# Regrouping normalised rows through DRAM and transposing them on VectorE, in a one-core transformer block kernel

## The chip, the cores and the metric

The kernel runs on one core of a Trainium2 chip. The metric is the device time of one execution in microseconds (us). Before the change it is 309.4 us, the median of 3 runs (308.99 to 310.95). A core has five engines with a queue of instructions each: TensorE (PE; its weight loads are shown as PEld), VectorE (DVE), ScalarE (ACT), GpSimd (POOL) and SyncE (SP). SP issues nearly all transfers of this kernel. Each engine takes its instructions in order, so an instruction that waits for a semaphore holds back all those behind it.

## The reference

x has 2048 rows (sequence) of 640 features, in bf16. The rows are normalised, and two branches work on the same normalised rows; the result is the sum of x and both.

```python
xn = _layernorm(x, axis=-1)
return x + _A_ref(xn, A_wqkv, A_wo) + _B_ref(xn, B_w_gate, B_w_up, B_w_down)
```

Branch A is attention with 32 heads of 20 features, where each query sees itself and the 255 keys before it, followed by a product with wo. Branch B is `(sigmoid(xn @ w_gate) * (xn @ w_up)) @ w_down` with 1536 hidden features. All the first products (q, k, v, gate, up) contract over the 640 features, so TensorE needs the normalised rows transposed: features on partitions, rows along the free axis.

## The kernel before

The sequence is cut into four chunks of 512 rows (CW), each chunk into four blocks of 128 rows (SBC). The transposed rows of a chunk are a tile `xnT` of 128 partitions x 5 slices (DC) x 512 rows. In the kernel before, slice d on partition p holds feature 128d + p, and the weights are loaded with the same order of their rows (L143, L182).

Chunk 0 is normalised and transposed at the start, with PE transposes (`transpose_rows`, L276 to L280). For chunks 1 to 3, `g_norms` (L343 to L359) is a generator: four steps of statistics on DVE (L252, L258), one power on POOL for all four blocks (L264), a gap of some steps, and four steps that normalise one block each on DVE (`norm_block`, L270). `turn_block` (L282) then gives each block to a transposing DMA on SP's queue, straight into `xnT`. Chunk 3 turns its blocks in a generator of its own (`g_turns`, L361).

The order of all work is laid down when the program is built. Attention steps (scores on PE L487, exponential on ACT L493, mask on POOL L504 or DVE L497, value product on PE L520, its transposes on DVE L532 and L548) come in a fixed list. Between them the class `Fill` (L551) pulls pieces of the other work out of a list of generators (L689 to L707), each with an estimated cost. `mix(a, b, first, every)` runs generator b beside a: from a's step `first` on, after each `every` of a's steps it takes one step of b. So the norms of chunk 1 run beside the gate and up products of chunk 0 ("gu0a", "gu0b"), those of chunk 2 beside the output product of chunk 0 ("out0"), and those of chunk 3 beside "gu1b" and "out1". Directly after each of these comes the q and k projection of the chunk ("qk1", "qk2", "qk3").

What stands on SP's queue around chunk 1 is, in this order: the four turns, the load of x for chunk 2 (`load_x(2)`, L140), eight transfers that turn wo inside DRAM (L212), five loads of wd (L205), two transfers that clear pads of the q and k scratch (L178), the stores of the q projection (L305, with the loads of wo, L217, after the fourth), the stores of the k projection (L305), and the loads that spread q and k over partitions (L315).

The buffers that matter:

- x of a chunk (`xc`) has one buffer for all chunks (pool `xp`, one buffer), read by the statistics and the norms.
- `st`, the projection results on their way to DRAM, has six buffers (pool `stp`); a chunk writes ten, five for q by DVE (L301) and five for k by ACT (L303).
- The accumulators of q, k, v, gate, up, the value product and the output product share four PSUM banks (pool `ps_d`); the scores have one tile of four banks (`ps_s`).
- The normalised block `xn` has four buffers.

Of the kernel before, what the change touches and what calls it, by code (L numbers as in the profile page):

```python
# [9 lines left out]
P = 128  # L10
S = 2048
D = 640
# [3 lines left out]
DC = D // P  # L16
FC = F // P
CW = 512
NCH = S // CW
SBC = CW // P  # L20
# [6 lines left out]
FS = 768  # L27
# [10 lines left out]
BF16 = mybir.dt.bfloat16  # L38
# [55 lines left out]
def kernel(  # L94
# [11 lines left out]
    nc = tc.nc  # L106
# [28 lines left out]
    xc = {}  # L135
# [4 lines left out]
        nc.sync.dma_start(out=t, in_=xr[:, c * SBC:(c + 1) * SBC, :])  # L140

    wqkv = [const.tile([P, DC, D], BF16, name="w" + part) for part in "qkv"]
    wqkv_r = A_wqkv.rearrange("(c p) n -> p c n", p=P)  # L143
    wg = [const.tile([P, DC, FS], BF16, name=f"wg{k}") for k in range(F // FS)]
    wu = [const.tile([P, DC, FS], BF16, name=f"wu{k}") for k in range(F // FS)]
    wd = const.tile([P, FC, D], BF16, name="wd")
# [32 lines left out]

    def load_gu(t, w, k, lo=0, hi=FS):  # L180
        nc.sync.dma_start(out=t[k][:, :, lo:hi],
                          in_=w.rearrange("(c p) f -> p c f", p=P)[:, :, k * FS + lo:k * FS + hi])  # L182

    load_gu(wg, B_w_gate, 0, 0, FS // 2)
    load_gu(wu, B_w_up, 0, 0, FS // 2)
    clear("q", 0)
    clear("k", 0)
    load_gu(wg, B_w_gate, 0, FS // 2)

    def load_rest():  # L190
# [30 lines left out]
    ident = const.tile([P, P], BF16, name="ident")  # L221
# [24 lines left out]
    xnT = {}  # L246
    xns = {}
# [13 lines left out]
    def ln_block(c, s, mv=None):  # L261
        return ln_mv(ln_half(c, s, 1, ln_half(c, s, 0)), mv)

    def rstd_blocks(mvs):  # L264
        rstds = lnp.tile([P, SBC], FP32, name="rstds", bufs=1)
        nc.gpsimd.tensor_scalar(out=rstds, in0=mvs[:, :, 1], scalar1=EPS, scalar2=None, op0=ADD)
        nc.gpsimd.tensor_tensor(out=rstds, in0=rstds, in1=neghalf, op=POW)
        return rstds

    def norm_block(c, s, mv, rstd):  # L270
        xn = lnp.tile([P, D], BF16, name="xn")
        nc.vector.tensor_scalar(out=xn, in0=xc[c][:, s, :], scalar1=mv[:, 0:1],  # L272
                                scalar2=rstd[:, 0:1], op0=SUB, op1=MULT)
        xns[c, s] = xn

    def transpose_rows(s, copy, lo=0, hi=DC):  # L276
        pt = ps_h.tile([P, DC, P], BF16, name="pt", tag="h")
        for d in range(lo, hi):
            nc.tensor.transpose(pt[:, d, :], xns[0, s][:, d * P:(d + 1) * P], ident)  # L279
        copy(out=xnT[0][:, lo:hi, s * P:(s + 1) * P], in_=pt[:, lo:hi, :])  # L280

    def turn_block(c, s):  # L282
        nc.sync.dma_start(out=xnT[c][:, :, s * P:(s + 1) * P], in_=xns.pop((c, s)), transpose=True)

    def new_xnT(c):
        xnT[c] = xtp.tile([P, DC, CW], BF16, name="xnT")
# [53 lines left out]

    MM = 216

    def g_norms(c, turn, gap=3):  # L343


        new_xnT(c)
        mvs = lnp.tile([P, SBC, nc.vector.BN_AGGR_DIM], FP32, name="mvs", bufs=1)
        for s in range(SBC):
            ln_block(c, s, mvs[:, s, :])
            if s == SBC - 1:  # L350
                rstds = rstd_blocks(mvs)
            yield 0
        for _ in range(gap):
            yield 0
        for s in range(SBC):
            norm_block(c, s, mvs[:, s, :], rstds[:, s:s + 1])
            yield 0
            if turn:
                turn_block(c, s)  # L359

    def g_turns(c):  # L361
        for s in range(SBC):
            turn_block(c, s)
            yield 0

    def g_qk(c):
        for w in "qk":
            for m in range(DC):
                proj_block(w, c, m)
                if c == 0 and w == "q" and m == 1:  # L370
                    load_x(1)
                if c == 0 and w == "q" and m == 3:
                    load_gu(wu, B_w_up, 0, FS // 2)
                if c == 1 and w == "q" and m == 3:
                    load_wo()
                if c and w == "k" and m == DC - 1:
                    spread("q", c, 0, GH)
                yield 5 * MM
        if c == 0:
            spread("q", c, 0, 2)  # L380
            spread("k", c, 0, 2)
            spread("q", c, 2, 4)
            spread("k", c, 2, 4)
# [19 lines left out]
    def part(w, d, f):  # L403
        k, first = divmod(f * P, FS)
        return w[k][:, d, first:first + P]

    def g_gu(c, f0, f1):
        for f in range(f0, f1):
            pg = ps_d.tile([P, CW], FP32, name="pg", tag="d")
            for d in range(DC):  # L410
                nc.tensor.matmul(pg, lhsT=part(wg, d, f), rhs=xnT[c][:, d, :],  # L411
                                 start=(d == 0), stop=(d == DC - 1))
            th = tp.tile([P, CW], FP32, name="th")
            nc.scalar.activation(out=th, in_=pg, func=TANH, scale=0.5)  # L414
            yield 5 * MM
            pu = ps_d.tile([P, CW], FP32, name="pu", tag="d")
            for d in range(DC):
                nc.tensor.matmul(pu, lhsT=part(wu, d, f), rhs=xnT[c][:, d, :],  # L418
                                 start=(d == 0), stop=(d == DC - 1))
            h = hp.tile([P, CW], BF16, name="h")  # L420
            ht[c, f] = h
            nc.vector.scalar_tensor_tensor(out=h, in0=th, scalar=1.0, in1=pu, op0=ADD, op1=MULT)  # L422
            yield 5 * MM
# [6 lines left out]
    def down(c, s, y, cut):  # L430
        for f in range(FC):
            nc.tensor.matmul(y[:, 0:cut[1] - cut[0]], lhsT=ht[c, f][:, s * P:(s + 1) * P],  # L432
                             rhs=wd[:, f, cut[0]:cut[1]], start=(f == 0), stop=False)
            if f % 6 == 5:
                yield 6 * 136
# [11 lines left out]
    def new_rows(c, s, name="rows", bufs=3, queue=nc.sync):  # L447
        rows = lnp.tile([P, D], BF16, name=name, bufs=bufs)
        queue.dma_start(out=rows, in_=xr[:, c * SBC + s, :])
        return rows  # L450
# [5 lines left out]
    def outp(c, s, ys, rows):  # L456
        for y, cut in zip(ys, HALVES):
            add_wo(c, s, y, cut)
        for y, cut in zip(ys, HALVES):
            add_x(y, cut, rows)  # L460
        store(c, s, rows)

    def g_out(c, between, ahead=()):
        nxt = new_rows(c, 0)
        for s in range(SBC):
            rows = nxt
            if s == 0:
                yield from ahead
            if s + 1 < SBC:
                nxt = new_rows(c, s + 1)  # L470
            ys = [ps_d.tile([P, CW], FP32, name=f"y{i}", tag="d") for i in range(2)]
            for y, cut in zip(ys, HALVES):
                yield from down(c, s, y, cut)
            if s == 0:
                yield from between
            outp(c, s, ys, rows)
            yield 10 * 136
# [117 lines left out]
    def mix(a, b, first, every=1, rest=True):  # L595

        for k, cost in enumerate(a):
            yield cost
            if k >= first and (k - first) % every == 0:
                yield next(b, 0)  # L600
        if rest:
            yield from b
# [39 lines left out]
    for lo, hi in ((0, 3), (3, DC)):  # L642
        transpose_rows(0, act, lo, hi)
    norm_act(1, xn1, neg1, r1)
    mv3 = ln_mv(ln_half(0, 3, 1, stats3))
    transpose_rows(1, dve)
    v00 = project_v(0, 0, 0)
    r3 = root(mv3)
# [3 lines left out]
    v10 = project_v(0, 1, 0)  # L652
    copy_v(0, 0, 0, v00, dve, (0,))
    transpose_rows(3, dve)
    v01 = project_v(0, 0, 1)
    norm_act(2, xn2, neg2, r2)
# [20 lines left out]
    fill = Fill()  # L677
    GU = 10 * MM
    OUT = 4 * 34 * 136
    APART = 1800  # L680
    FIRST_PART = 1000
    def later(load, *args):
        load(*args)
        yield 0

    norms1 = g_norms(1, True)
    norms2 = g_norms(2, True)
    norms3 = g_norms(3, False, 6)
    fill.add("gu0a", mix(g_gu(0, 0, 4), norms1, 4, 1, False), 4 * GU)  # L689
    fill.add("gu0b", mix(g_gu(0, 4, 12), norms1, 0), 8 * GU)  # L690
    fill.add("x2", later(load_x, 2), 0)
# [7 lines left out]
    fill.add("qk2", g_qk(2), 50 * MM)  # L699
    fill.add("v2", mix(g_v(2), g_gu(1, 3, 7), 0, 1), 40 * 136 + 4 * GU)  # L700
    fill.add("gu1b", mix(g_gu(1, 7, 12), norms3, 0, 1, False), 5 * GU)
    fill.add("out1", mix(g_out(1, g_gu(2, 0, 1)), itertools.chain(norms3, g_turns(3)), 1, 2), OUT + GU)
    fill.add("qk3", g_qk(3), 50 * MM)
    fill.add("v3", mix(g_v(3), g_gu(2, 1, 5), 0, 1), 40 * 136 + 4 * GU)
    fill.add("gu2", g_gu(2, 5, 12), 7 * GU)
# [13 lines left out]
    for t, (c, k, o, step) in enumerate(todo):  # L719
# [11 lines left out]
        pt, late = scores(c, o, step)  # L731
# [12 lines left out]
    c = NCH - 1  # L744
# [6 lines left out]
    rows = [new_rows(c, s, *home, queue=nc.scalar) for s, home in enumerate(homes)]  # L751
# [55 lines left out]
```

## Time and profile before

| | us |
|---|---|
| median of 3 runs | 309.4 |
| lowest and highest run | 308.99, 310.95 |
| span of the profiled execution, first to last instruction | 307.5 |
| PE busy | 299.6 |
| ACT busy | 198.4 |
| DVE busy | 170.7 |
| POOL busy | 169.3 |

The profiled execution's own time is known by its span alone; what lies around the span, start and end of the execution, is not shown, and the median lies 1.9 us above it. The profile's page gives the busy time of each engine, the span in 40 slices, the chain of work that ended last and the costliest groups of instructions. A timeline line gives the start, the length, the engine, the line in the code, the operation, output and inputs, shapes, the number of instructions merged into the line, and in brackets the idle time before it with what ended it. "SPq" marks the issue of a transfer on SP's queue: the length there is that of the issue, not of the transfer.

### The profile page before, as it was taken

To read this page: it belongs to the slowest core of one execution; us is meant where nothing else is said; L and a number is where in the kernel's file an instruction comes from. 1 tells how busy PE (TensorE), PEld (TensorE's weight loads), DVE (VectorE), ACT (ScalarE), POOL (GpSimd) and SP (SyncE) were. 2 spreads that over 40 slices of the span, in tenths; PEclk is the share of its full clock that TensorE was granted. 3 is DMA by queue.
4 is the path that set the end of the run, shared out by engine and by line. 5 is a ranking of instruction groups with operands and counts; after the bars stand their busy time and mean duration, and the time that the engine had idled before them with its cause. 6 is when DMAs were issued, how large, how long until landed. Compare 5 with 4: busy or idle time off the path is not lost.

```text
span 307.5 us, 9944 instructions
## 1 busy us (share of the span) xinstructions
PE 299.6 (97%) x4276; PEld 167.5 (54%) x4311; DVE 170.7 (56%) x339; ACT 198.4 (65%) x197; POOL 169.3 (55%) x308
## 2 busy tenths in 40 slices
PE   7999999999999999999999999999999999999995
PEld 3654444555657654554457654554546664444774
DVE  5633666639698364487946164392824536363523
ACT  6933877698855649888674547878585547687000
POOL 6000686787874828576683729467372937566000
PEclk9999999999999999999999999999999999999999
DMA  7997976986407352820002712730000200000202
GB/s 215 366 344 236 324 158 214 337 238 209 154 2 139 58 179 68 272 83 2 3 3 67 129 58 87 250 122 0 5 0 2 87 26 21 2 2 7 83 21 67
DMA packets 40460, 35.68 MB, mean 116 GB/s; under 512 B 10560, under 2 KB 39872, under 8 KB 40384
## 3 DMA queue, kind: packets, MB, share of 16 engines
q1 hardware_dynamic: 39552, 34.27, 37.3%
q10 hardware_dynamic: 864, 0.77, 0.9%
q8 instruction: 34, 0.56, 0.8%
q14 instruction: 10, 0.08, 0.1%
HBM read 23.63 MB, written 10.26 MB: 110 GB/s over the span
## 4 chain that ended last, share of the span: by engine, by line
PE 96%; issue 1%; DMA 1%; DVE 1%; ACT 0%; SPq 0%
PE y L432 18%; PE pu L418 17%; PE pg L411 17%; PE pqk L297 14%; PE ps L487 9%; PE pv L326 7%; PE y L439 7%; PE acc L520 6%; DMA xc<-in_A_x_dram 1%; PE pt L279 0%; ACT xn L617 0%; DVE xn L272 0%; DVE xn L628 0%; SPq L156 0%; DVE stats L252 0%
## 5 line engine op out<-in xcount | busy, mean ns | idle before, releaser
L504 POOL TENSOR_SCALAR_AFFINE_SELECT pT<-pT 64x512 bf16<-64x512 bf16 (+1 forms) x256 | 157.7, 616 | 108.1 <-ACT pT L493 95.6
L493 ACT ACTIVATE pT<-ps 128x2048 bf16<-128x2048 f32 (+1 forms) x76 | 141.0, 1855 | 59.6 <-PE ps L487 54.6
L422 DVE SCALAR_TENSOR_TENSOR h<-th,pu 128x512 bf16<-128x512 f32 x48 | 32.8, 684 | 52.6 <-PE pu L418 46.1
L418 PE MATMUL pu<-xnT,wu 128*128 128x512 bf16 x228 | 59.0, 380 | 0.7 <-issue 0.2
L411 PE MATMUL pg<-xnT,wg 128*128 128x512 bf16 x226 | 58.5, 380 | 0.9 <-issue 0.3
L432 PE MATMUL y<-wd,h 128*128 128x320 bf16 (+2 forms) x396 | 56.7, 295 | 0.0
L432 PEld LDWEIGHTS <-h 128*128 128x128 bf16 x396 | 36.7, 98 | 15.8 <-issue 2.0
L414 ACT ACTIVATE th<-pg 128x512 f32<-128x512 f32 x48 | 28.6, 595 | 15.5 <-PE pg L411 15.4
L411 PEld LDWEIGHTS <-wg 128*128 128x128 bf16 x240 | 22.2, 98 | 25.8 <-issue 1.8
L418 PEld LDWEIGHTS <-wu 128*128 128x128 bf16 x240 | 22.0, 98 | 25.5 <-issue 2.0
L487 PE MATMUL ps<-qT,kT 20*64 20x320 bf16 (+4 forms) x1440 | 32.1, 260 | 0.0
L532 DVE STREAM_TRANSPOSE t<-acc 128x512 f32<-128x512 f32 x32 | 21.1, 697 | 19.7 <-PE acc L520 19.7
L487 PEld LDWEIGHTS <-kT 20*64 20x64 bf16 x1440 | 15.4, 103 | 24.9 <-issue 21.8
L443 DVE SCALAR_TENSOR_TENSOR rows<-y,rows 128x320 bf16<-128x320 f32 x30 | 14.4, 488 | 25.5 <-PE y L439 25.3
L544 DVE TENSOR_TENSOR on<-t,rec 128x320 bf16<-128x320 f32 (+4 forms) x48 | 27.8, 580 | 1.1
L326 PE MATMUL pv<-wv,xnT 128*128 128x320 bf16 x160 | 25.7, 300 | 0.0
L439 PE MATMUL y<-wo,oc 128*128 128x320 bf16 (+2 forms) x165 | 24.2, 295 | 0.0
L297 PE MATMUL pqk<-xnT,wk 128*128 128x512 bf16 x97 | 23.1, 381 | 0.2
L297 PE MATMUL pqk<-xnT,wq 128*128 128x512 bf16 x94 | 22.8, 381 | 0.4 <-issue 0.2
L335 DVE CAST v<-pv 64x320 bf16<-64x320 f32 x29 | 14.1, 486 | 12.5 <-PE pv L326 12.3
L520 PE MATMUL acc<-pT,v 64*32 64x320 bf16 (+4 forms) x1440 | 19.7, 253 | 0.0
L520 PEld LDWEIGHTS <-v 64*32 64x32 bf16 x1440 | 16.2, 91 | 5.8 <-ACT pT L493 1.7
(50 smaller groups left out, 178.7 us busy)
## 6 DMA issues: line engine op xcount, KB each, us to landing
qT<-sq SPq DMA_DIRECT2D x16, 256.0 KB
kT<-sk SPq DMA_DIRECT2D x16, 256.0 KB
sq<-st SPq DMA_DIRECT2D x20, 128.0 KB
sk<-st SPq DMA_DIRECT2D x20, 128.0 KB
out_dram<-rows SPq DMA_DIRECT2D x15, 160.0 KB
wg<-in_B_w_gate_dram SPq DMA_DIRECT2D x4, 480.0 KB
wu<-in_B_w_up_dram SPq DMA_DIRECT2D x4, 480.0 KB
xc<-in_A_x_dram SPq DMA_DIRECT2D x3, 640.0 KB
```

The costliest lines, as they stand in the source:

```text
L297: nc.tensor.matmul(ps, lhsT=wt[:, m, :], rhs=xnT[c][:, d, :], start=(d == 0), stop=(d == DC - 1))
L326: nc.tensor.matmul(ps[:, 0:HALF], lhsT=xnT[c][:, d, s * P:(s + 1) * P], rhs=wqkv[2][:, d, hf * HALF:(hf + 1) * HALF], start=(d == 0), stop ...
L411: nc.tensor.matmul(pg, lhsT=part(wg, d, f), rhs=xnT[c][:, d, :], start=(d == 0), stop=(d == DC - 1))
L414: nc.scalar.activation(out=th, in_=pg, func=TANH, scale=0.5)
L418: nc.tensor.matmul(pu, lhsT=part(wu, d, f), rhs=xnT[c][:, d, :], start=(d == 0), stop=(d == DC - 1))
L422: nc.vector.scalar_tensor_tensor(out=h, in0=th, scalar=1.0, in1=pu, op0=ADD, op1=MULT)
L432: nc.tensor.matmul(y[:, 0:cut[1] - cut[0]], lhsT=ht[c, f][:, s * P:(s + 1) * P], rhs=wd[:, f, cut[0]:cut[1]], start=(f == 0), stop=False)
L439: nc.tensor.matmul(y[:, 0:cut[1] - cut[0]], lhsT=oc[c, m][:, s * P:(s + 1) * P], rhs=wo[:, m, cut[0]:cut[1]], start=False, stop=(m == DC - 1))
L487: nc.tensor.matmul(ps[a * U:(a + 1) * U, i, col * U:(col + n) * U], lhsT=qk["k", kc, o // GH][32 * i:32 * i + DH, o % GH + a, kb * U:(kb + ...
L493: nc.scalar.activation(out=pt[:, :, 0:width], in_=ps[:, :, 0:width], func=EXP, scale=SCALE)
L504: nc.gpsimd.affine_select(out=view, in_=view, pattern=[[0, HG], [0, n], [sign, U]], compare_op=GE, fill=0.0, base=base, channel_multiplier ...
L520: nc.tensor.matmul(acc[32 * i:32 * i + 32, q * U:(q + n) * U], lhsT=vt[kb][a * U:(a + 1) * U, u, h * VW:h * VW + 32], rhs=pt[a * U:(a + 1) ...
```

## The change

The transposed rows of chunks 1 to 3 are made in another way, and the order of the features changes: slice d on partition p now holds feature 5p + d. The weights wqkv, w_gate and w_up are loaded in that order, and the PE transposes of chunk 0 read every fifth feature.

For a later chunk, `put_block` stores each normalised block to a scratch in DRAM (two scratches, taken in turn). After the fourth, `regroup` loads it back in four transfers into the chunk's own x buffer `xc`: partition 32b + j gets, for each of the 16 groups t of 32 rows, row 32t + j and its features 160b to 160b + 159, in runs of 320 bytes. Then five instructions on DVE (`turn`, one per slice) transpose 32x32 blocks, reading every fifth element, and write one slice of `xnT` each, 128 x 512. `g_norms` yields `lag` steps between regroup and the turns and one step after each turn. On DVE the turns of chunk 1 stand around the last three h products of chunk 0 (one, two, two), those of chunk 2 around the third pair of row additions of "out0" (one before, four after), those of chunk 3 before, between and after the last two pairs of "out1" (two, two, one). The order on PE, ACT and POOL is that of before.

```diff
-    wqkv_r = A_wqkv.rearrange("(c p) n -> p c n", p=P)
+    wqkv_r = A_wqkv.rearrange("(p c) n -> p c n", c=DC)
...
-                          in_=w.rearrange("(c p) f -> p c f", p=P)[:, :, k * FS + lo:k * FS + hi])
+                          in_=w.rearrange("(p c) f -> p c f", c=DC)[:, :, k * FS + lo:k * FS + hi])
...
-            nc.tensor.transpose(pt[:, d, :], xns[0, s][:, d * P:(d + 1) * P], ident)
+            nc.tensor.transpose(pt[:, d, :], xns[0, s].rearrange("p (i d) -> p d i", d=DC)[:, d, :], ident)
...
-    def turn_block(c, s):
-        nc.sync.dma_start(out=xnT[c][:, :, s * P:(s + 1) * P], in_=xns.pop((c, s)), transpose=True)
+    xs = [tc.dram_tile([CW, D], BF16, name=f"xs{k}") for k in range(2)]
+
+    def put_block(c, s):
+        nc.sync.dma_start(out=xs[c % 2][s * P:(s + 1) * P, :], in_=xns.pop((c, s)))
+
+    def regroup(c):
+
+        rows = xs[c % 2].rearrange("(t j) (b f) -> b j t f", j=32, b=4)
+        for b in range(4):
+            nc.sync.dma_start(out=xc[c][32 * b:32 * b + 32].rearrange("j s (a f) -> j (s a) f", a=4), in_=rows[b])
+
+    def turn(c, d):
+        nc.vector.transpose(out=xnT[c][:, d, :], in_=xc[c].rearrange("p s (t d) -> p d (s t)", d=DC)[:, d, :])
...
-    def g_norms(c, turn, gap=3):
-
-
-        new_xnT(c)
+    def g_norms(c, gap=3, lag=3):
...
             norm_block(c, s, mvs[:, s, :], rstds[:, s:s + 1])
+            put_block(c, s)
             yield 0
-            if turn:
-                turn_block(c, s)
-
-    def g_turns(c):
-        for s in range(SBC):
-            turn_block(c, s)
+        regroup(c)
+        for _ in range(lag):
+            yield 0
+        new_xnT(c)
+        for d in range(DC):
+            turn(c, d)
             yield 0
...
-    norms1 = g_norms(1, True)
-    norms2 = g_norms(2, True)
-    norms3 = g_norms(3, False, 6)
+    norms1 = g_norms(1)
+    norms2 = g_norms(2)
+    norms3 = g_norms(3, 6, 2)
...
-    fill.add("out1", mix(g_out(1, g_gu(2, 0, 1)), itertools.chain(norms3, g_turns(3)), 1, 2), OUT + GU)
+    fill.add("out1", mix(g_out(1, g_gu(2, 0, 1)), norms3, 1, 2), OUT + GU)
```

## The prediction

> **What bounds the kernel now.** I read the page's busy times and clock first, then the chain of work that ended last.
>
> ```profile
> span 307.5 us, 9944 instructions
> PE 299.6 (97%) x4276; PEld 167.5 (54%) x4311; DVE 170.7 (56%) x339; ACT 198.4 (65%) x197; POOL 169.3 (55%) x308
> PEclk9999999999999999999999999999999999999999
> PE 96%; issue 1%; DMA 1%; DVE 1%; ACT 0%; SPq 0%
> ```
>
> TensorE is busy 97% at full clock, and the chain runs through it for 96%. The table of windows gives PE 264.9 of the 267 us from 13 to 280, so at most 2.1 us are left to win there. The order on PE, ACT and POOL is the same in both kernels. So the change can only matter by making PE wait, and a wait of PE is paid in full. Next I read the stretch where chunk 1 is normalised, turned and projected: first the timeline of the SP queue, then DVE, then ACT and PE.
>
> ```profile
> 39.32 5.27 SPq L283 DMA_TRANSPOSE xnT<-xn  x4
> 44.64 0.70 SPq L140 DMA_DIRECT2D xc<-in_A_x_dram  x1
> 45.40 5.04 SPq L212 DMA_DIRECT2D wo_i<-in_A_wo_dram  x8
> 50.48 4.34 SPq L205 DMA_DIRECT2D wd<-in_B_w_down_dram  x5
> 55.19 0.60 SPq L178 DMA_DIRECT2D sq<-kT  x1
> 56.15 0.56 SPq L178 DMA_DIRECT2D sk<-kT  x1
> 57.24 5.30 SPq L305 DMA_DIRECT2D sq<-st  x4
> 62.60 2.07 SPq L217 DMA_DIRECT2D wo<-wo_i  x4
> 64.76 0.53 SPq L305 DMA_DIRECT2D sq<-st  x1
> ```
>
> One queue, in order: the load of x chunk 2 at 44.64 stands ahead of 3.6 MB of loads and pads, and these stand ahead of chunk 1's q stores.
>
> ```profile
> 50.31 0.29 DVE L544 TENSOR_TENSOR on<-t,rec 128x128 bf16<-128x128 f32 x1
> 50.52 0.68 DVE L422 SCALAR_TENSOR_TENSOR h<-th,pu 128x512 bf16<-128x512 f32 x1
> 51.79 0.69 DVE L422 SCALAR_TENSOR_TENSOR h<-th,pu 128x512 bf16<-128x512 f32 x1 [0.59 <-PE pu L418]
> 54.57 0.69 DVE L422 SCALAR_TENSOR_TENSOR h<-th,pu 128x512 bf16<-128x512 f32 x1 [2.09 <-ACT th L414]
> ```
>
> Here the five new transposes of chunk 1 go: one before the first of these h, two before the second, two before the third.
>
> ```profile
> 65.43 1.08 ACT L303 CAST st<-pqk 128x512 bf16<-128x512 f32 x2
> 66.37 1.92 ACT L493 ACTIVATE pT<-ps 128x2048 bf16<-128x2048 f32 x1
> 68.14 1.12 ACT L303 CAST st<-pqk 128x512 bf16<-128x512 f32 x2
> 69.95 1.88 ACT L493 ACTIVATE pT<-ps 128x2048 bf16<-128x2048 f32 x1 [0.69 <-PE ps L487]
> ```
>
> ```profile
> 68.35 1.04 PE L520 MATMUL acc<-pT,v 64*32 64x320 bf16 x72
> 69.32 0.43 PE L487 MATMUL ps<-qT,kT 20*64 20x320 bf16 x24
> 69.68 0.58 PE L326 MATMUL pv<-wv,xnT 128*128 128x320 bf16 x3
> ```
>
> The cast at 65.43 writes the seventh st tile of the chunk. The pool has six, so it needs the buffer of the first q store. The trace's completion events put that store's landing at about 64.5 (its semaphore's next user goes out at 64.76): 0.9 us of slack now.
>
> **Removed.** Twelve transposing transfers. Each holds SP 1.2 us and lands 2.6 to 3.3 us after its issue; for chunk 1 the last lands near 46.5, eight us before its first reader (54.59). PE waits for none of them: gain 0.
>
> **Put and regroup.** The 160 KB stores of rows to DRAM (L454) land 1.8 to 2.0 us after issue, so the fourth put of chunk 1, issued when the last norm ends (42.65), lands at 44.6. The first regroup then goes out and lands like the loads from DRAM (2.2 to 3.0 us in the completion events), about 47.3. The other three follow at a rate that no row shows for 320 B runs. Nearest: wo<-wo_i, also 32 partitions, 200 KB in 0.95 us, so 0.76 for 160 KB; upper, 32 packets per engine at the 46 ns that the 1024 B packets take, 1.5. I take 0.95, between the two and nearer to the row of the same shape: the last lands at 50.15, or 7.5 us after the last put's issue. DVE comes to the first transpose at 50.5: no wait (with 1.5: 1.3 us).
>
> [...]
>
> **Transposes on DVE.** L548, the same operation and shape with contiguous input, takes 0.71 us, and L532 shows pairs at 0.65 spacing. Here the input steps 5 elements. The nearest strided row is the weight load: L297 (step 5) 119 ns against 98, +21%. Lower end 0.65, upper 0.86; a far end, reciprocals over a strided column (239 ns for 16 against 164 for 1), would give 2.6 us. I take 0.65 apart, the row of the operation itself. Seven instructions (five transposes, two h) from 50.5 end at 55.1. The q matmuls of chunk 1 start at 54.59 and need the fifth slice at 55.45: no PE wait. The h products come 0.7 to 1.5 us late, and the banks they free are wanted later than that.
>
> [...]
>
> **The wait that is added on SP.** The x buffer is one tile, and regroup now refills it. So the load of x chunk 2 waits for the fifth transpose: 55.1 instead of 44.64, 10.5 us later. Everything queued behind it is as late: wo_i, wd, the pads (these have slack: wd is read at 82.2, wo at 88.6), and the q stores. The first q store lands at 64.5 + 10.5 = 75.0, less 0.3, since no transposing transfer is still ahead of the load (5.05 us to landing at 44.64, 4.74 for the one at 108.49): 74.7. ACT's cast at 65.43 then starts at 74.8. Behind it on ACT: second cast to 75.9, exponential to 77.8, two casts to 78.9. PE stops at 68.35 for its banks (L520), then at 69.32 for the score banks, which the exponential frees at 77.8. 77.8 − 69.3 = **8.5 us**. ACT has almost no idle time until 82, so nothing of it comes back. Late next: k for chunk 1 is spread about 81 and lands near 84.7; its first scores are due at 78.0 + 8.5 = 86.5.
>
> Low end of this term: if the x load and what follows (4.2 MB) drained at the best rate shown (363 GB/s from 54 to 58), 11.6 us, plus 2 us for the store, the landing is at 68.8 and PE loses some 2.6.
>
> **Chunk 2.** The last norm ends at 98.15, so the last regroup lands at 98.2 + 7.5 = 105.7, while DVE reaches the transpose at 101.2. It waits 4.5 us; behind it stand two row additions, whose banks the q projection needs at 107.4. Transpose to 106.4, rows to 107.25, four transposes to 109.85. The fifth slice was needed at 108.24: **1.7 us** of PE. The next x load waits behind the last rows anyway. With 0.76 per regroup it is 1.1, with 1.5 it is 3.4.
>
> **Chunk 3.** Last norm 162.4, regroup done at 170.0. The fifth transpose stands behind the rows at 178.07 and ends at 179.2; needed 179.18: **0.2**.
>
> **Start.** The 20 weight loads of the PE transposes get the step of 5: 20 × 21 ns = 0.4 at most, part beside matmuls: **0.2**. The weights are cut into the same runs (640 to 1280 B): 0.
>
> Sum: 8.5 + 1.7 + 0.2 + 0.2 = 10.6. The profiled span becomes 318.1; the median of 309.4 lies 1.9 above the span and I keep that: **320.0 us**.
>
> **Rivals.**
> 1. Regroup or transposes dearer: 1.5 us per regroup adds 1.3 in chunk 1 and 1.7 in chunk 2, 323.0; with transposes 21% slower, ten times 0.15 more, 324.5. For it: small runs into 32 partitions. Against: 0.95 for 200 KB on the same partitions. The far price of 2.6 us would add about 20.
> 2. The delayed loads drain faster: 2.6 + 1.7 + 0.4 = 4.7, 314.1. For it: DMA stands idle before 55. Against: the wo_i transfers crawl on few engines (210 GB/s at 50 to 54 against 363 after), and they are the same.
> 3. The queue's delay is hidden, because the load finds another buffer or the slack is larger: 1.7 + 0.4, 311.5. That would be the change not making the load wait. Against: the x pool has one buffer.
> 4. Faster: without four transposing transfers (5.3 us of SP) the load of x chunk 2 leaves earlier, and with it all behind. It decides only if the transposes were done before 44.6, and the first cannot start before 50.5; even then PE has 2.1 us to give: 307.3 at best.
>
> **Chances.** Forecast (317.5 to 322.5) 0.62; rival 1 0.18, its far price 0.03 more; rival 2 0.12; rival 3 0.03; rival 4 0.02. A measurement of this kernel can tell about 1%, 3.1 us, so slower by more is 0.62 + 0.18 + 0.03 + 0.12 = 0.95, within 0.03, faster 0.02 (rival 4, if PE's idle time is more than I count). The range leaves out the far price, rivals 3 and 4: 314 to 326.
>
> **What would show it.** The x load of chunk 2 at about 55 on SP, behind the fifth transpose; PE idle of 8 us near 68 to 78, released through ACT's casts of st; DVE idle of about 4.5 us before the first transpose of chunk 2 and PE short by under 2 us at its q projection; transposes of 0.71 us. I am wrong if the stores of q go out near 57, if the transposes take over 1 us, or if DVE waits for the regroup of chunk 1.

## The result and the profile after

The changed kernel takes 323.25 us, the median of 4 runs (321.99 to 324.33), against 309.37 (308.99 to 310.95): the ratio is 1.0444, with an interval of 1.0407 to 1.048. It is 13.9 us slower; the forecast was 10.6 slower, 320.0, in a range of 314 to 326. The profiled execution of the changed kernel is the longest of its four, with 324.33 us of its own time and a span of 322.6, so its trace has 15.1 us to explain.

The page of the changed kernel, the lines that answer to those of before (busy times, granted clock, chain of work that ended last):

```profile
span 322.6 us, 10010 instructions
PE 307.8 (95%) x4311; PEld 169.3 (52%) x4311; DVE 180.1 (56%) x354; ACT 198.5 (62%) x197; POOL 168.3 (52%) x308
PEclk9999999996999997999999999999999999999999
PE 81%; DMA 10%; SPq 3%; DVE 3%; issue 1%; ACT 0%; DVEq 0%; ACTq 0%
```

PE's share of the chain falls from 96% to 81%, and DMA and SP's queue take its place. PE's busy time is 8.2 us longer, but the trace of before has 35 fewer matmul records for the same products, so that row says little. The clock row says more: it has a 6 and a 7 where it was full before. The records of the granted clock give 0.5 from 74.45 to 81.28 and from 122.24 to 125.65 us, and 1 otherwise; in the kernel before it is 1 throughout.

PE does the same work in the same order in both kernels. So the start of the same instruction in both traces shows where time was lost. I take the first value product (`acc`) of an attention step as the mark:

| stretch on PE | before, us | after, us | added |
|---|---|---|---|
| span's start to the mark at 44.38 / 44.93 | 44.38 | 44.93 | 0.55 |
| on to the mark at 68.35 / 77.30 (chunk 1's q and k, and the stop) | 23.97 | 32.37 | 8.40 |
| on to 95.17 / 106.08 (what runs behind the stop) | 26.82 | 28.78 | 1.96 |
| on to 112.27 / 127.21 (chunk 2's first q products) | 17.10 | 21.13 | 4.03 |
| on to the last mark, 287.28 / 302.29 | 175.01 | 175.08 | 0.07 |
| sum | | | 15.01 |

The mark at 68.35 is where the stop begins, and a second wait can stand right behind it: the scores, for the tile that ACT's exponential frees. So I also give the start of these scores, 69.32 before and 79.57 after. Up to there 9.70 us are added (10.25 less the 0.55 of the start), and from there to the mark at 95.17 / 106.08 another 0.66 (25.85 before, 26.51 after).

The SP queue of the changed kernel around chunk 1, from its timeline:

```profile
39.86 3.65 SPq L285 DMA_DIRECT2D xs<-xn  x4
46.16 2.87 SPq L291 DMA_DIRECT2D xc<-xs  x4
56.77 0.40 SPq L140 DMA_DIRECT2D xc<-in_A_x_dram  x1
57.21 5.45 SPq L212 DMA_DIRECT2D wo_i<-in_A_wo_dram  x8
62.71 4.47 SPq L205 DMA_DIRECT2D wd<-in_B_w_down_dram  x5
...
69.41 3.88 SPq L316 DMA_DIRECT2D sq<-st  x4
...
76.64 0.52 SPq L316 DMA_DIRECT2D sq<-st  x1
```

The load of x for chunk 2 (L140) goes out at 56.77 instead of 44.64, after the fifth transpose, and all behind it is as late: the q stores start at 69.41 instead of 57.24. The next lines are DVE's, ACT's and PE's in the same stretch, from their timelines.

```profile
52.24 0.75 DVE L294 STREAM_TRANSPOSE xnT<-xc 128x512 bf16<-128x512 bf16 x1 [1.10 <-DMA xc<-xs]
...
53.49 1.38 DVE L294 STREAM_TRANSPOSE xnT<-xc 128x512 bf16<-128x512 bf16 x2
...
55.37 1.38 DVE L294 STREAM_TRANSPOSE xnT<-xc 128x512 bf16<-128x512 bf16 x2
```

```profile
64.55 0.59 ACT L314 CAST st<-pqk 128x512 bf16<-128x512 f32 x1 [0.70 <-PE pqk L308]
65.03 1.88 ACT L502 ACTIVATE pT<-ps 128x2048 bf16<-128x2048 f32 x1
76.66 1.07 ACT L314 CAST st<-pqk 128x512 bf16<-128x512 f32 x2 [9.74 <-DMA sq<-st]
77.62 1.90 ACT L502 ACTIVATE pT<-ps 128x2048 bf16<-128x2048 f32 x1
```

```profile
67.44 2.35 PE L308 MATMUL pqk<-xnT,wk 128*128 128x512 bf16 x10
77.30 2.28 PE L529 MATMUL acc<-pT,v 64*32 64x320 bf16 x72 [7.50 <-ACT st L314]
79.57 0.65 PE L496 MATMUL ps<-qT,kT 20*64 20x320 bf16 x24
```

Read from the last fence back to the first: PE stops 7.50 us until ACT empties a bank, ACT's cast waits 9.74 us until the first q store frees its st buffer, and that store was issued at 69.41. When PE goes on, it goes on slowly: the same 72 value products take 2.28 us, and took 1.04 before. This is the half clock. But the exponential behind the casts ends at 79.52 (77.62 + 1.90), and the scores start at 79.57: products at full clock would have had to wait for it there. The last view is chunk 2, on DVE and PE.

```profile
117.37 0.77 DVE L294 STREAM_TRANSPOSE xnT<-xc 128x512 bf16<-128x512 bf16 x1 [5.26 <-DMA xc<-xs]
118.06 0.85 DVE L452 SCALAR_TENSOR_TENSOR rows<-y,rows 128x320 bf16<-128x320 f32 x2
118.83 2.62 DVE L294 STREAM_TRANSPOSE xnT<-xc 128x512 bf16<-128x512 bf16 x4
```

```profile
122.16 5.12 PE L308 MATMUL pqk<-xnT,wq 128*128 128x512 bf16 x15
```

DVE waits 5.26 us for the regroup, PE then follows the transposes product by product, and the next 15 q products take 5.12 us, against 3.43 before: 1.69 of the 4.03 us are again the clock.

### The profile page after: what moved, and what is told of

Read it like the earlier page. It is cut to its first block, busy times and chain, and to the rows that moved or that the text cites. A ratio compares the mean times of both kernels' runs of the same rounds, so it can differ in the third digit from the quotient of the medians.

```text
span 322.6 us, 10010 instructions
## 1 busy us (share of the span) xinstructions
PE 307.8 (95%) x4311; PEld 169.3 (52%) x4311; DVE 180.1 (56%) x354; ACT 198.5 (62%) x197; POOL 168.3 (52%) x308
## 4 chain that ended last, share of the span: by engine, by line
PE 81%; DMA 10%; SPq 3%; DVE 3%; issue 1%; ACT 0%; DVEq 0%; ACTq 0%
PE pu L427 15%; PE pg L420 15%; PE y L441 15%; PE pqk L308 11%; PE ps L496 7%; PE pv L337 7%; PE y L448 6%; PE acc L529 6%; DMA xc<-xs 2%; DMA wo_i<-in_A_wo_dram 2%; DMA sq<-st 2%; DMA xs<-xn 2%; DMA wv<-in_A_wqkv_dram 2%; DVE xnT L294 2%; SPq L212 1%
## 5 line engine op out<-in xcount | busy, mean ns | idle before, releaser
L427 PE MATMUL pu<-xnT,wu 128*128 128x512 bf16 x240 | 59.8, 380 | 0.0
L420 PE MATMUL pg<-xnT,wg 128*128 128x512 bf16 x240 | 59.8, 380 | 0.0
L529 PE MATMUL acc<-pT,v 64*32 64x320 bf16 (+4 forms) x1440 | 20.9, 259 | 7.5 <-ACT st L314 7.5
L308 PE MATMUL pqk<-xnT,wq 128*128 128x512 bf16 x100 | 26.0, 401 | 2.0 <-DVE xnT L294 1.9
L529 PEld LDWEIGHTS <-v 64*32 64x32 bf16 x1440 | 16.9, 93 | 13.8 <-ACT st L314 8.4
L314 ACT CAST st<-pqk 128x512 bf16<-128x512 f32 x20 | 11.2, 603 | 17.1 <-DMA sq<-st 9.7
```

The source lines that it names most:

```text
L308: nc.tensor.matmul(ps, lhsT=wt[:, m, :], rhs=xnT[c][:, d, :], start=(d == 0), stop=(d == DC - 1))
L529: nc.tensor.matmul(acc[32 * i:32 * i + 32, q * U:(q + n) * U], lhsT=vt[kb][a * U:(a + 1) * U, u, h * VW:h * VW + 32], rhs=pt[a * U:(a + 1) ...
```

## The experiments

The theory under test: the regroup reuses the x buffer, so the next x load waits on SP, the q stores wait behind it, and ACT and PE wait for those (about 8.5 us); chunk 2's regroup costs 1.7; and a stop of PE is followed by a stretch at half clock that the forecast had not priced. The rivals: the loss lies in the transposes, the small runs or the new weight layout.

### Moving the held load out of the way

```diff
-    fill.add("x2", later(load_x, 2), 0)
...
+                if c == 1 and w == "k" and m == 0:
+                    load_x(2)
```

> The changed kernel, with one thing moved: the load of x for chunk 2 is issued between the first and the second store of the k projection of chunk 1, instead of directly behind the regroup. All else stays, transposes and regroup too. Theory (the load waits on SP for the fifth transpose, holds back the q stores, ACT waits for an st buffer, PE for its banks): the PE idle time of 7.5 us near 70 to 77 and the half clock after it go, the cast of the second k block starts within 2 us of its place in the kernel before, and the time falls by about 9.6, from 323.2 to 313.6. Rival (the regroup's own traffic and the DVE transposes delay chunk 1): the time stays within 1.5 of 323.2. The wait of chunk 2 (PE idle near its q projection, then half clock) stays in both.

Measured: 313.16 us (311.83 to 314.99), ratio 1.0126 (1.008 to 1.0173), with the transposes, the regroups and the layout all in place. Its SP queue and PE:

```profile
60.43 4.67 SPq L316 DMA_DIRECT2D sq<-st  x4
...
68.53 0.52 SPq L316 DMA_DIRECT2D sq<-st  x1
69.16 0.55 SPq L316 DMA_DIRECT2D sk<-st  x1
69.76 0.58 SPq L140 DMA_DIRECT2D xc<-in_A_x_dram  x1
```

```profile
70.31 1.04 PE L531 MATMUL acc<-pT,v 64*32 64x320 bf16 x72
```

The stop is gone and the value products take 1.04 us again. By the marks it adds 1.96 us at the start, 0.00 and 0.20 in the two stretches of chunk 1, 1.68 in chunk 2 and 0.06 behind. So where one load stands on one queue is worth 10.1 us of the 13.9. The 1.68 in chunk 2, at full clock, is the forecast's 1.7.

### The held load in the kernel before

```diff
+        if c == 1:
+            for _ in range(8):
+                yield 0
+            nc.vector.tensor_copy(out=scr, in_=xc[c][:, 0, 0:1])
+            yield 0
```

> The kernel before, with its transposing transfers, plus one copy of 128x1 elements on DVE that reads the x buffer of chunk 1 behind the third h product of the gate and up stretch (about 55.3 us), so that the load of x for chunk 2 must wait until then. No regroup, no DVE transposes. Theory (the held load alone makes the stall): the load leaves at about 55.4 instead of 44.6, the first q store lands at about 75, PE is late by 8.5 at the scores near 69, and 0.7 more because it then runs at half the granted clock for some us: 309.4 + 9.2 = 318.6. Rival (the stall needs the new transfers and transposes): 309.4 to 310.5.

Measured: 319.63 us (319.18 to 319.87), ratio 1.033 (1.0297 to 1.0364). One copy of one column that reads the x buffer late makes the kernel before 10.3 us slower, with the transposing transfers still in it. Its ACT and PE:

```profile
75.14 1.07 ACT L303 CAST st<-pqk 128x512 bf16<-128x512 f32 x2 [9.40 <-DMA sq<-st]
```

```profile
75.78 2.27 PE L525 MATMUL acc<-pT,v 64*32 64x320 bf16 x72 [7.16 <-ACT st L303]
```

The same wait, and the same value products at half clock. By the marks the stop costs 7.35 us (75.78 − 44.46 − 23.97) and what runs behind it 2.94, with the clock at 0.5 for 10.2 us; chunk 2 costs nothing here. Taken at the scores (78.05, against 69.32), the wait costs 8.65, where 8.5 was expected, and what runs behind it 1.64, where 0.7 was expected for the half clock. So the total came out 1.0 above the expectation by the term for the clock.

### More st buffers

```diff
-    stp = pool("stp", 6)
+    stp = pool("stp", 9)
```

> The changed kernel with nine buffers for st instead of six (room for ten is not there). SP's queue is as late as in the changed kernel; only what waits for it changes: the seventh to ninth st tile of chunk 1 find a free buffer, the tenth (fifth k cast on ACT) still needs the first q store to have landed, at 76. Theory (PE stands because ACT waits for an st buffer, and the place of that wait sets the loss): ACT's wait moves from the second to the fifth k cast, PE gets through the value product and the scores behind it and stops at the second v product instead, for 5.5 us instead of 7.5, and the time falls by about 2.3 to 321. Rival (PE would wait for the late q and k tiles anyway, the st buffers only show it first): 323.2, with PE standing at the first scores of chunk 1.

Measured: 320.68 us (319.13 to 322.65), ratio 1.0387 (1.0346 to 1.0427), 2.6 us less than the changed kernel. ACT now gets three casts further, and waits at the tenth; PE runs past the value products and stops at the scores of the next attention step (the second v product was expected, for 5.5 us):

```profile
68.24 0.63 ACT L314 CAST st<-pqk 128x512 bf16<-128x512 f32 x1
74.90 0.59 ACT L314 CAST st<-pqk 128x512 bf16<-128x512 f32 x1 [6.04 <-DMA sq<-st]
```

```profile
77.32 0.55 PE L496 MATMUL ps<-qT,kT 20*64 20x320 bf16 x16 [4.93 <-ACT pT L502]
```

So the st pool decides when the stop comes, and the late store how long it lasts. By the marks chunk 1 costs 7.80 us here and 10.36 in the changed kernel. Of the 7.80, 5.00 are added up to the scores at 77.32 (72.22 before) and 2.80 behind them, with the clock at 0.5 for 6.8 us: part of what the shorter wait saves goes back to the clock. Chunk 2 cost 1.72 at full clock in this execution. No run has a tenth st buffer, or a tile of its own for the regroup, which would be as large as five of them.

### The weight layout alone

```diff
-    wqkv_r = A_wqkv.rearrange("(c p) n -> p c n", p=P)
+    wqkv_r = A_wqkv.rearrange("(p c) n -> p c n", c=DC)
...
-            nc.tensor.transpose(pt[:, d, :], xns[0, s][:, d * P:(d + 1) * P], ident)
+            nc.tensor.transpose(pt[:, d, :], xns[0, s].rearrange("p (i d) -> p d i", d=DC)[:, d, :], ident)
```

The gate and up weights are loaded in the new order as well; the rest is the kernel before. The run leaves out the matching order of the rows in chunks 1 to 3, so its sums there are over mismatched features; the work is the same.

> The kernel before, with the new order of the weights' rows (partition p holds rows 5p to 5p+4) and the PE transposes of chunk 0 reading every fifth feature; chunks 1 to 3 keep the transposing transfers of whole blocks, so there the slices of x and the weights' rows do not belong together (the sums are over mismatched features; the work is the same). Theory (the layout costs only the start, where PE stood 0.55 later at its first q product in the changed kernel): 309.4 + 0.2 to 0.6. Rival (the weight loads run slower in the new layout, which in the changed kernel brought the spread of k three us later and the regroup with it): 311 or more, and the last load of the up weights lands after 41 instead of 38.3.

Measured: 309.5 us (309.18 to 310.31), ratio 1.0005 (0.9989 to 1.002). The layout and the stepped weight loads cost nothing that can be told.

### Holding the clock up

Here constant products keep PE busy: 34 ahead of chunk 1's last block of five k products and 10 ahead of chunk 2's first block of q products, into the bank that the real products then overwrite.

```diff
+WARM = {("k", 1, DC - 1): 34, ("q", 2, 0): 10}
...
+        for _ in range(WARM.get((w, c, m), 0)):
+            nc.tensor.matmul(ps, lhsT=ones[:, 0:P], rhs=ones, start=True, stop=True)
```

> The changed kernel plus 44 matmuls of 128x512 over a constant whose results are overwritten: 34 ahead of the fifth k product of chunk 1 and 10 ahead of the first q product of chunk 2. They fill the two PE waits with work (34 x 0.216 = 7.3 us, 10 x 0.216 = 2.2 us) and shorten no wait. Theory (part of the loss, which the forecast left out, is the granted clock of 0.5 for 6.8 us after the first wait and 3.4 us after the second): the clock stays at 1.0, the 15 q products behind the second wait take 3.4 us instead of 5.1, the products behind the first save about 0.7, and the time falls by 2.4 to 320.8. Rival (the half clock is hidden by other engines, the whole loss is waiting): 323.2, or above it by what the added matmuls overhang, up to 1.

Measured: 325.14 us (324.7 to 327.13), ratio 1.0522 (1.048 to 1.0564): the total missed the expectation by 4.3. By the marks, chunk 1 (both stretches) is 1.68 us shorter than in the changed kernel and chunk 2 1.85, at full clock. PE at chunk 1 and at chunk 2:

```profile
77.11 1.33 PE L532 MATMUL acc<-pT,v 64*32 64x320 bf16 x72
79.22 0.43 PE L499 MATMUL ps<-qT,kT 20*64 20x320 bf16 x24 [0.78 <-ACT pT L505]
```

```profile
121.00 3.43 PE L311 MATMUL pqk<-xnT,wq 128*128 128x512 bf16 x15
```

So the clock was a cost of its own, but a small one in chunk 1. Of the 1.68, 0.87 lies ahead of PE's restart, where PE ran at full clock or stood in both kernels: this execution was 0.68 later at the first mark, and the wait took that up. At full clock PE then waits 0.78 us for ACT's exponential, as the forecast had it. From the scores to the next mark it takes 25.86 us, against 26.51 in the changed kernel and 25.85 in the kernel before; so the half clock cost 0.66 behind chunk 1's stop, and the rest of the 1.96 is a wait that stays at full clock.

The total rose all the same: 4.01 us are lost between the marks at 210.94 and 233.07, where neither kernel loses any: PE stops for 2.28 us inside a block of v products, with nothing that it waits for ("issue"), and then runs at half clock from 217.7 to 221.2. The page lists a DMA queue of the kind "instruction", q8, with 34 packets and 0.56 MB, which is 16 KB each; in the trace's DMA records one of them comes at 214.0 us, just when the transfers that spread q and k of chunk 3 are through. From 210 to 215 the DMA engines were 95% busy. The 44 constant products had moved all later code by 88 instructions (10098 in this trace, 10010 in the changed kernel's). The guess that the next three runs test is that q8 brings PE's code and that PE stood for it; no record says what PE stood for.

Ten constant products alone, in chunk 2:

```diff
+WARM = {("q", 2, 0): 10}
```

> The changed kernel with ten matmuls over a constant (results overwritten) ahead of the first q product of chunk 2, and none in chunk 1. In the run with both sets the two stretches came out 2.85 us shorter on PE's timeline, but PE then stood 2.3 us near 214 with nothing to wait for that the profile shows, and ran at half clock after it, so the total rose. Theory (the half clock behind the wait of chunk 2 costs 1.7 to 1.9 us by itself; the stop near 214 belongs to where the added instructions put the loading of PE's code): here the code moves by a quarter as much, the stop does not come, and the time is 321.4. Rival (the half clock costs nothing in the end): 323.2 or more without such a stop.

Measured: 323.49 us (322.4 to 324.51), ratio 1.0456 (1.0422 to 1.0489): no gain, so the expectation was missed. The 15 q products do take 3.43 us again, but by the marks chunk 2 gains only 0.37 on the changed kernel: the regroup landed 9.4 us after the last put's issue in this execution (8.2 in the changed kernel's), and PE waited 1.3 us ahead of the constant products. What runs behind chunk 1's stop is 1.21 longer, with the half clock falling otherwise, and the stretch around 214 is 0.75 longer. This run settles nothing alone.

The shift of the code without constant products: the first nine feed-forward blocks of chunk 0 are multiplied in two halves of 256 columns, which makes 45 products more over the same columns (ten products of 256 took 1.25 to 1.27 us in the last of the three runs, five of 512 took 1.24).

```diff
+        n = 2 if left[0] > 0 else 1
+        left[0] -= 1
+        for i in range(n):
+            cut = slice(i * CW // n, (i + 1) * CW // n)
+            for d in range(DC):
+                nc.tensor.matmul(ps[:, cut], lhsT=part(w, d, f), rhs=xnT[c][:, d, cut],
+                                 start=(d == 0), stop=(d == DC - 1))
```

> The changed kernel, with the first nine feed-forward blocks of chunk 0 multiplied in two halves of 256 columns each: 45 products become 90, the work of TensorE stays the same, and every later instruction of TensorE stands about 90 places further on in its code. In the run with constant products TensorE stopped for 2.28 us at 214 us, in the second v product behind the spreads of chunk 3, while a 16 KB packet of instruction code came at 214.0 us, when the spreads had just drained. Theory A, the fetch of TensorE's code is held up behind the spreads, and the shift of the code by some 88 instructions is what made the fetch late: the stop comes here too, 2 us or more near 214 us, with half the clock behind it, and the time is 326 to 327.5 us. Theory B, the stop came from the constant products themselves or by chance: no stop of more than 0.3 us there, and the time is that of the changed kernel, 322.5 to 324 us.

Measured: 326.09 us (323.31 to 327.98), ratio 1.0531 (1.0469 to 1.0594). PE, ahead of the stop and at it:

```profile
214.41 0.43 PE L337 MATMUL pv<-wv,xnT 128*128 128x320 bf16 x2
217.62 0.57 PE L337 MATMUL pv<-wv,xnT 128*128 128x320 bf16 x3 [2.78 <-issue]
218.03 1.52 PE L424 MATMUL pg<-xnT,wg 128*128 128x512 bf16 x5
```

The stop is there, in the same block of v products, with the q8 packet at 215.3 (217.5 in the changed kernel, where nothing stops) and slow products behind it (1.52 us for five gate products, 1.24 elsewhere); by the marks the stretch takes 22.63 us, 4.51 more than in the changed kernel. So it comes without the constant products too, and what theory A foretold came in this execution; that late code is its cause, no record shows. One of the four took 323.31, as theory B had it, so the stop may not come each time (that one has no trace).

The same split in 42 blocks, together with all 44 constant products, moves the code by 508 instructions. That is about two packets, an estimate from the 34 q8 packets and the 8622 products and weight loads of PE in the changed kernel's trace: 254 each, if the packets hold nothing else (this run's page has 35):

```diff
+    left = [42]
...
+WARM = {("k", 1, DC - 1): 34, ("q", 2, 0): 10}
```

> The run with 34 constant products ahead of chunk 1's last k product and 10 ahead of chunk 2's first q product, and besides with the first 42 feed-forward blocks of chunks 0 and 1 multiplied in two halves: 210 more products and as many more weight loads, so that with the 44 constant ones the code behind them is shifted by 508 instructions, about two packets of 16 KB, and the fetches should fall near the spreads of chunk 3 as they did in the changed kernel, where nothing stopped. Theory A (late code): no stop at 214 us, and the saving of the constant products shows in the total, 323.3 less 2.9, so 320 to 321.5 us. Theory B (the constant products themselves or chance): the stop stays, 324.5 to 326 us.

Measured: 324.33 us (323.91 to 324.77), ratio 1.0485 (1.0453 to 1.0518). The page's clock row and PE where time is lost:

```profile
PEclk9999999999999999999999999999999999999999
```

```profile
79.58 0.43 PE L506 MATMUL ps<-qT,kT 20*64 20x320 bf16 x24 [0.78 <-ACT pT L512]
145.77 0.41 PE L506 MATMUL ps<-qT,kT 20*64 20x320 bf16 x18
147.77 0.23 PE L506 MATMUL ps<-qT,kT 20*64 20x64 bf16 x6 [1.59 <-issue]
```

The stop at 214 is gone, as theory A had it. The total of 320 to 321.5 did not come, since PE stopped once more, for 1.59 us with nothing that it waits for, while a q8 packet came at 145.3 us behind the spreads of chunk 2 (a DMA share of 1.01 in the table of windows from 142 to 144, and of 0.00 from 146 to 148). In this stop and in the two near 214, PE went on 2.3 to 2.5 us after the packet began (147.77, 216.46, 217.62). By the marks 2.0 us were saved up to 125.17, and 1.9 lost again up to 160.17. Of the 2.0, 0.57 lie behind the scores of chunk 1 and 1.48 in chunk 2; the scores themselves start at 79.58, as in the changed kernel at half clock (79.57). The saving of the clock never reached a total in these runs; it stands on the marks alone.

### Giving the regroup more time

```diff
-    norms2 = g_norms(2)
+    norms2 = g_norms(2, 3, 8)
...
-    fill.add("v1", mix(g_v(1), g_gu(1, 0, 2), 1, 2), 40 * 136 + 2 * GU)
+    fill.add("v1", mix(mix(g_v(1), g_gu(1, 0, 2), 1, 2), norms2, 4, 1, False), 40 * 136 + 2 * GU)
```

This comes on top of the later load.

> The kernel with the x load moved (313.2) and, besides, the statistics and norms of chunk 2 begun in the stretch of the v projection of chunk 1, about 10 us earlier, with a lag of 8 steps instead of 3 between regroup and transposes. Theory (what is left in chunk 2 is DVE waiting for the regroup with the last four transposes behind it, 1.7 us of PE): DVE no longer waits there, PE passes from the output product into the q projection without a gap, 313.2 - 1.7 = 311.5. Rival (the five transposes themselves are too much for DVE in that stretch): PE still waits over 1 us there, 312.5 or more.

Measured: 311.2 us (311.17 to 312.63), ratio 1.007 (1.0044 to 1.0097). By the marks chunk 2 adds 0.00 now, but the stretch ahead of it adds 1.40, where the later load alone adds 0.20; and the start adds 0.76, there 1.96. So most of what this run won over the later load lies at the start, which the edit does not touch: the edit took 1.68 away in chunk 2 and put 1.20 ahead of it, and that the total meets the expected 311.5 is in part luck.

```diff
-    norms1 = g_norms(1)
+    norms1 = g_norms(1, 3, 5)
```

With chunk 1's norms two steps earlier as well:

> As the last, and the statistics and norms of chunk 1 two steps earlier as well, with a lag of 5 instead of 3. Theory (the rest in chunk 1 is the regroup that lands 1.1 us after DVE wants it, 0.76 us on PE): 311.5 - 0.8 = 310.7, at most 0.5% above the kernel before; what stays is the start. It does not beat the kernel before, since nothing that PE waited for is taken away. Rival (regrouping and transposing cost PE something that no wait shows): 311.5 or more.

Measured: 311.02 us (310.15 to 313.34), ratio 1.0062 (1.004 to 1.0085). It can't be told from the run ahead of it, and by the marks chunk 1 adds 0.36 up to its value product here (0.05 in the run ahead), so the earlier norms won nothing that shows. No version beats the kernel before, whose PE had 2.1 us of idle time to give.

## Why the forecast was right, and where it fell short

The mechanism held: the x load waits for the transposes, the q stores behind it, ACT for st, PE for ACT, and the later load and the held load show it from both sides. The size was short. 323.25 lies outside the forecast's own band of 317.5 to 322.5, and the range of 314 to 326 holds it by the room left for dearer regroups and transposes (323.0 to 324.5). What came instead were the half clock and a regroup that set out later; that these are about as large is luck.

**The wait added on SP: right path, 1.2 too small.** The forecast's 8.5 us are counted at the scores, from 69.32 to 77.8; there the changed kernel added 9.70. The chain is the one forecast: load, queue, q store, st buffer, ACT's cast, exponential, PE. But the x load left at 56.77 (55.1 forecast): 0.55 for the later start and 1.10 for the first transpose, which waited for the regroup. The same two, added to the 77.8 forecast for the exponential's end, give 79.45; it ended at 79.52. The kernel before with the load held, which has no regroup, added 8.65. The later load takes the term out.

**Chunk 1's regroup: put at nothing, and 1.1 of the 1.2.** I had DVE at its first transpose with no wait, and named a wait there as a sign of being wrong. It waited 1.10 us, and the queue carried that on to the q stores. The last put landed 2.96 us after its issue at 43.2, not 1.9, and the DMA engines were 99% busy from 40 to 42. With nine st buffers they were 84% busy then, the put landed 1.8 us after its issue, and DVE didn't wait; nor did it with the later load, and with the split of 45 it waited 1.87. So this wait changes from execution to execution.

**Chunk 2: right at full clock.** Forecast 1.7; 1.68 with the later load, 1.72 with nine st buffers, 1.51 with the split of 45. In the profiled execution of the changed kernel it was 2.34 without the clock: there the last regroup landed 8.2 us after the last put's issue (7.5 forecast; 7.4 to 7.6 in the runs with 9 buffers, with constant products and with the split of 45). The first regroup transfer went out 2.88 us after that put, and 1.9 to 2.0 in those runs; a rows load that stands between them on SP took 1.51 us to issue, against 0.42 with nine buffers.

**Chunk 3 and start.** Chunk 3: 0.2 forecast, 0.07 at most. Start: 0.2 forecast, 0.55 found, as PE waited 0.33 us for wv to land. That wait was 0.91 and 1.73 in two other runs and nothing in a third, so it belongs to the execution; the layout by itself cost nothing.

**The step that failed: the sum prices a stop of PE at its length.** "A wait of PE is paid in full" was too little. It took all work behind the stop at the durations of before. In the changed kernel the granted clock fell to 0.5 at both stops, from 74.45 and from 122.24 us. Behind chunk 1's stop that cost 0.66, since the slow value products ran while PE would have waited for the exponential anyway; in chunk 2, where nothing hides it, it cost 1.69. These 2.35 us, with 1.20 more in the wait added on SP, 0.35 more at the start and 0.64 more in chunk 2, less 0.13 in chunk 3, are 4.4: the 15.0 us of the profiled execution against the 10.6 forecast. The median lies 1.1 below that execution. The mean granted clock was 0.984 in three of the four executions, 0.989 in the shortest (321.99 us): 10 us at half clock and 7. So the clock term is not the same in all; what else differed, no trace shows.

The half clock lasted 6.83 us at the stop of 7.50 us and 3.41 us in chunk 2. How long PE had been idle does not settle whether it comes: in chunk 2 PE was busy 2.46 of the 4.00 us from 118 to 122, near 214 single stops of 2.28 and 2.78 us were enough, and the single stop of 1.59 us with the longer shift was not. With nine st buffers and the split of 45, chunk 2 kept the full clock; there PE was busy 2.74 and 2.95 of its emptiest 4.00 us. What decides whether the half clock comes, these runs don't show.

**Rival 1, dearer regroup or transposes: fell.** Its time, 323.0, is nearer to the result than the forecast, but its prices are not there. DVE did wait longer than forecast for the regroup in both chunks (about 1.1 and 0.64 on PE), mainly because the regroup set out later. The regroups took 0.93 us each in chunk 2 (0.95 forecast), and single transposes took 0.75 to 0.77 us, in pairs 0.69 each, against 0.71 for contiguous input. The packets of 320 bytes took 26 ns in the mean, those of 1024 bytes 50: a byte of the short ones took 1.7 times as long. So the short runs lost rate, but not the half that 1.5 us would be: 0.93 per regroup (the packets of all four start between 112.94 and 116.66), against 0.76 scaled from the wo row. Why they lose it, no run here shows. Rival 2 fell, since the delayed transfers took as long as before: 12.6 us from the x load's issue to the first q store's, in both kernels. Rival 3 failed with the single x buffer, and rival 4 with it.

## What to carry to other kernels

When an in-place reuse of a buffer gives a load a new wait, look at what stands behind that load on its queue: here 10 of 14 us came from stores that had nothing to do with the change, and moving one load by a few places took them away. Price a stop of PE at its length and, where it is as long as those here (2.28 to 7.50 us), at 0.7 to 2.8 us more for what was added behind it, and a short, broken stop at its length and between nothing and 1.69 us more (chunk 2's): an estimate from these runs. Before charging a slow clock for a stretch, look whether PE would have waited there anyway: here two thirds of what seemed to be clock behind the long stop was another wait. Where an experiment adds instructions to an engine, look for new stops far behind the edit (here 2.28 and 2.78 us near 214) before reading its total.

## What the runs showed of the hardware

- Around each stop of PE of 2.28 to 7.50 us (seven of them) the granted clock fell to 0.5 for 3.4, 6.8 or 10.2 us; after one of 1.59 us it did not. Behind four of them 72 value products took 2.27 to 2.28 us, not 1.04. What was added behind the stop, up to the next mark, was 0.66 to 2.80 us. A stop in pieces, 1.54 us of 4 (the changed kernel's chunk 2), was enough once; 1.05 and 1.26 us of 4 (nine st buffers and the split of 45) and a single 1.31 us (ten constant products) were not.
- The changed kernel's page lists a DMA queue of the kind "instruction", q8: 34 packets of 16 KB, 0.7% of the 16 DMA engines' span. That they hold PE's code is an inference from their coming earlier when PE's instructions are added ahead of them (217.5, then 214.0 and 215.3); no record says whose they are. Three of them, at 145.3, 214.0 and 215.3, came at stops of PE of 1.59, 2.28 and 2.78 us with nothing to wait for, at 145.3 and 214.0 behind transfers that kept the DMA engines 95% busy or more. But in the changed kernel packets came at 146.90 and 217.49 behind a DMA share of 1.06 and 1.02 (the 4 us ahead of each), and PE was busy all of the 2.5 us behind each. So that such a packet, held up by the transfers, is what stops PE is not shown. Cutting 45 products of chunk 0 in two brought one such stop and 4.51 us; a further shift took it away and met another.
- Reading every fifth bf16 element cost VectorE's 128x512 transpose at most 0.06 us of 0.71.
